# A rewritten head order, carried products over four quarters of the array, and moved transfers in a linear-attention and mixer kernel

## The chip, the cores and the metric

The kernel runs on one core of a Trainium2 chip. The metric is the device time of one execution in microseconds. TensorE (PE) multiplies, VectorE (DVE), ScalarE (ACT) and GpSimd (POOL) do the elementwise work, SyncE (SP) issues nearly all transfers, in the order of its queue.

## The reference

Three stages follow each other on 4 batches of 768 tokens with 8 heads of 48 values:

```
f = 1 / (1 + exp(-f_logit))
state = f[t] * state + k[t] (outer) v[t];  y[t] = q[t] @ state        # attention, per head
xn = (x - mean) / sqrt(var + 1e-6) * g_ln;  x = x + relu(xn @ w_ch1) @ w_ch2        # first block
h = relu(x.T @ w_tok1) @ w_tok2;  u = x + h.T                         # second block, token mixing
out = u + relu(u @ w_ch1') @ w_ch2'                                   # second block, channels 384 -> 1536 -> 384
```

Weights and activations are split into a high and a low part, and each product is made of three (high x high, high x low, low x high).

## The kernel before

**Attention** is cut into 24 chunks n of 128 tokens; chunk n has batch n mod 4 and place c = n div 4 in its sequence, so chunks 0 to 3 have no old state. The steps of a chunk are named in the order list: `lf`, `lq`, `lv` load, `log` takes the logarithm of the gate, `cum` sums it on TensorE (from chunk 8 `scan` does it on VectorE), `ek` and `eq` are the factors for K and Q, `km` and `qm` the products with them, `kp` transposes K on TensorE and `kt` copies it, `sc` are the scores, `st` the new state, `A0` and `A1` the masked scores, `stm` the state at the chunk's middle, `ste` and `std` the state at its end, `y` (L441) the products inside a half chunk, `z` (`outp2`) the **carried** products of Q with the old and the middle state (L432), `lna`, `lnc`, `lnv`, `lnr` the normalisation, `tp`, `ah`, `al` the transposed result in two parts. Scores, new states and outputs of a chunk lie in one pair of PSUM banks (`t["sc"]`). An output half i are 64 tokens and 64 of the array's columns; a row half r are four heads and 64 of the array's rows.

**First block.** Three chunks make a step `m0` to `m7` with 12 groups of 9 products of 384 columns (`m0.5`; `h` and `l` are its two parts) and 12 groups of the second layer (`m0.o21`; `r` adds and `d` stores the result). The weights `w0` to `w23` are loaded (`ld`), converted on VectorE (`a`, `b`, `c`) and split (`h`, `l`); later weights `s0`, `s1`, ... go through memory.

**Second block.** R (L852) and H (L874) are the token mixing, each with a tile `ts` of 256 KB from memory in two buffers; G (L932) and O (L985) are the two channel layers, O with weights in `w2h` and `w2l`, which `weights4` reloads in four pairs of 576 KB. `weights3` loads the six groups of G's weights. Checks of all weights (`cs`, L1137 to L1143) are strewn over the block at `spots`.

**The order.** Every step is entered in `Slots` with a slot number, and each engine runs its steps in the order of these numbers. Up to slot 77 the order is written out by hand in `ORDER`; a step `2.cum+11` issues 11 products of zeros ahead of itself into its own bank (`busy`, L540, 224 columns), and `1.y+10` issues 3 x 10 narrow ones (L449, 64 columns). `POOL` names the steps that GpSimd does in place of VectorE, `OTHER` the copies that change between ScalarE and VectorE, `AT` the results that go to the fourth one-bank buffer.

Of the kernel before, what the change touches and what calls it, by code (L numbers as in the profile page):

```python
# [51 lines left out]
ORDER = """
    0.lf 2.lf 0.log 1.lf 0.lq 2.log 3.lf 0.cum 2.cum+11 0.eq 0.ek 1.log 1.lq 0.lv 3.log 0.qm 0.km 1.cum+24 0.kp
    1.ek 0.kt 0.tot 2.eq 1.km 0.sc 0.st 0.A0 0.A1 3.cum 1.kp w14.ld w5.ld w5.a 2.ek 1.eq 0.y 0.stm 0.yw 1.qm 0.z
    1.kt 3.ek 2.tot 0.lna 1.sc 1.lv w14.a w5.b w5.c 1.tot w14.b 0.ste 0.std 5.lf 2.lq 0.lnc 1.st 1.A0 5.log w14.c
    0.tp+10 1.A1 1.y+10 2.km 5.cum 3.tot 1.stm 2.qm 2.lv 0.ah 1.yw 1.ste 1.z 3.lq 0.al 2.kp 3.km 2.sc 1.std 2.kt
    2.st 3.eq w14.h 4.lf 2.A1 6.lf 2.A0 3.qm 3.kp w14.l 1.lna 5.ek 1.lnc 4.log 5.tot w2.ld 2.y+6 2.stm w2.a 3.lv
    2.ste 3.kt w5.h w2.b 4.cum 6.log 1.tp 4.lq 3.sc 3.st 4.tot 3.A1 1.ah 4.eq 3.A0 w5.l 2.yw 2.z 2.std 1.al 3.y+9
    4.ek 2.lna 3.yw 3.stm 3.z 7.lf 2.lnc w4.ld 3.ste 7.log 4.qm 5.eq w4.a w2.c 4.km 4.kp 4.sc+4 w4.b w4.c 4.kt
    3.lna 4.lv w3.ld 3.lnc 4.st 2.tp 7.cum w4.h 4.A1 2.ah 7.ek 1.lnv 5.lq 6.cum w4.l w0.ld 3.tp 4.A0 8.lf 2.al 4.y  # L60
    4.stm 7.eq 7.tot w2.h 4.ste m0.4 5.km w3.a 4.yw 2.lnv 5.kp w1.ld w0.a 5.qm 5.lv 3.ah 5.kt w3.b w0.b w2.l 3.al
    w3.c w17.ld 4.z 5.sc 4.lna m0.5 5.st 6.eq 6.ek 6.tot w0.c w1.a w3.h w1.b 6.lq w0.h 5.A0 5.A1 m0.2 0.lnv w3.l
    w13.ld 5.y w1.c w17.a 3.lnv m0.3 5.yw m0.h5 w12.ld 9.lf w10.ld 6.lv 7.lv 5.stm m0.h4 m0.h2 6.km 4.lnc m0.l5
    m0.l4 5.z m0.l2 w1.h w1.l 5.lna 5.ste w0.l 6.qm 4.tp+7 5.lnc 6.kp 4.ah m0.0 4.al 5.tp 6.kt 5.lnv w17.b w13.a
    w13.b 6.sc w17.c m0.1 w13.c 5.ah w13.h 5.al w16.ld w12.a m0.h0 m0.h3 m0.h1 6.st m0.l3 9.log m1.2 w13.l w16.a
    m0.l1 w19.ld m1.1 8.log w17.h m1.h2 7.lq w12.b m1.0 w16.b m0.l0 w12.c 7.qm 6.A0 m1.l2 w17.l w15.ld m1.3 m1.h0
    7.km w18.ld m1.h1 w12.h 8.scan m1.h3 m1.l1 m1.l0 m1.5 7.kp m1.h5 7.kt w12.l 6.A1 w15.a m1.l5 7.sc m1.4 6.y
    w15.b w16.c 4.lnv w18.a w15.c w7.ld m1.o20 m1.o10 6.stm w18.b 8.lv 7.st 6.yw w16.h w15.h m1.h4 m1.l3 6.z 2.lnr
    m1.o00 w9.ld w15.l w18.c m1.l4 w19.a 8.tot w16.l 8.lq w8.ld 6.lna m0.o00 w10.a w19.b w19.c w10.b 6.ste 9.scan
    6.lnc w6.ld m1.o01 8.ek w18.h m1.o21 10.lv w19.h 7.A0 w10.c 5.lnr m1.o11 w18.l w19.l 3.std m0.o01 8.eq w9.a  # L70
    w6.a 7.A1 w22.ld m1.r01 m1.r11 7.y w10.h w6.b 10.lf w10.l w7.a m0.r01 w7.b w7.c w6.c w7.h 7.stm 8.km 8.qm
    m0.o20 9.ek w6.h 7.yw m0.o10 w11.ld m0.o21 10.log 7.z w7.l 8.kp w8.a 10.scan 8.kt w6.l m1.r21 m0.o11 9.tot
    w8.b 9.eq 7.lna w9.b 9.lq w8.c w11.a w9.c 7.ste 8.sc m0.7 11.lf w21.ld w20.ld w8.h 9.km m0.h7 m0.10 m0.r11
    m0.r21 w8.l w9.h m0.6 m0.h10 m0.l7 w11.b m1.6 m0.8 7.lnc 11.log w9.l w20.a w11.c m0.l10 w22.a m0.h6 8.st
    w23.ld w22.b w20.b w11.h m1.7 w22.c s0.ld m0.h8 m1.h6 m0.l6 w11.l 11.scan m0.l8 m0.9 w20.c w21.a 8.A0 m1.l6
    m0.h9 m0.l9 4.std m0.11 w22.h 10.eq w21.b 7.tp 7.ah m1.10 8.A1 8.stm 7.al w22.l w23.a w20.h m0.h11 s1.ld 9.lv
    8.y w20.l 11.lv 8.yw m1.h7 m1.11 m0.l11 m1.l7 w23.b 9.kp w23.c s0.a 8.z m1.8 m1.h10 10.lq 6.std 9.kt m1.h11
    9.qm w23.h 10.tot m1.h8 w21.c w23.l w21.h m1.l10 w21.l 7.lnv 8.lna 9.sc m1.l8 m0.o12 5.std 6.tp 8.lnc m1.l11
    11.eq m1.9 9.st 6.ah 6.lnv m1.h9 8.ste 9.A0 m1.l9 s2.ld 8.tp m0.o13 8.ah 10.ek 9.A1 m1.o02 9.y 9.stm s1.a 6.al
    m0.r13 s0.b 8.lnv s0.c 10.km 8.al m1.o03 9.yw m1.r03 9.z m0.o02 10.qm m0.o22 10.kp 11.ek m0.d1 10.sc 10.kt  # L80
    m0.o23 m0.o03 10.st m1.o12 11.lq 10.A0 9.lna 9.ste m1.o22 m0.r23 m1.o13 m0.r03 9.lnc 10.stm 10.ste 9.std s1.b
    7.std s0.h s1.c 10.std m1.r13 m1.d1 m0.d2 8.std m1.d0 m0.d0 s3.ld m1.o23 10.A1 8.lnr
""".split()
# [1313 lines left out]
```

## Time and profile before

| | |
|---|---|
| Time, median of 3 runs | 768.1 us (765.84 to 770.25) |
| Profiled execution | 766.76 us, span 765.0 us |
| PE busy | 751.5 us (98%), 7080 instructions |
| DVE busy | 503.2 us (66%) |
| ACT busy | 355.3 us (46%) |
| POOL busy | 126.5 us (17%) |
| Chain that ended last | PE 92%, DVE 3%, DMA 2%, ACT 1%, issue 1% |
| Granted TensorE clock | 0.999 of 2.4 GHz on the mean |

Matmuls are pipelined and the ends of their records are modelled, so TensorE counts as busy also where it starts its next product late; what counts is from start to start.

### The profile page before, as it was taken

To read this page: it belongs to the slowest core of one execution; us is meant where nothing else is said; L and a number is where in the kernel's file an instruction comes from. 1 tells how busy PE (TensorE), PEld (TensorE's weight loads), DVE (VectorE), ACT (ScalarE), POOL (GpSimd) and SP (SyncE) were. 2 spreads that over 40 slices of the span, in tenths; PEclk is the share of its full clock that TensorE was granted. 3 is DMA by queue.
4 is the path that set the end of the run, shared out by engine and by line. 5 is a ranking of instruction groups with operands and counts; after the bars stand their busy time and mean duration, and the time that the engine had idled before them with its cause. 6 is when DMAs were issued, how large, how long until landed. Compare 5 with 4: busy or idle time off the path is not lost.

```text
span 765.0 us, 17368 instructions
## 1 busy us (share of the span) xinstructions
PE 751.5 (98%) x7080; PEld 733.0 (96%) x7080; DVE 503.2 (66%) x920; ACT 355.3 (46%) x891; POOL 126.5 (17%) x108
## 2 busy tenths in 40 slices
PE   9899999999999999999999999999999999999997
PEld 8789999999999999999999899999999999999996
DVE  3889793787786776576245464867558663868481
ACT  6675343353545545443232342654347443656440
POOL 1334333024133330010000000101000000101010
PEclk9999999999999999999999999999999999999999
DMA  8675542467565675553349864344243534343401
GB/s 264 186 232 162 178 129 66 150 195 232 172 208 177 190 218 162 171 167 128 124 118 362 312 238 138 104 152 162 84 124 100 170 127 138 104 142 99 131 21 68
DMA packets 61561, 122.54 MB, mean 160 GB/s; under 512 B 6944, under 2 KB 27808, under 8 KB 60704
## 3 DMA queue, kind: packets, MB, share of 16 engines
q1 hardware_dynamic: 61472, 121.33, 50.5%
q8 instruction: 58, 0.95, 0.5%
q14 instruction: 31, 0.25, 0.1%
HBM read 96.93 MB, written 24.38 MB: 159 GB/s over the span
## 4 chain that ended last, share of the span: by engine, by line
PE 92%; DVE 3%; DMA 2%; ACT 1%; issue 1%; SPq 0%; DVEq 0%
PE mo L985 19%; PE mm L582 19%; PE mo L612 18%; PE mm L932 16%; PE rt L852 3%; PE ht L874 3%; PE sc L432 2%; DMA ts<-t_d 2%; PE sc L441 2%; PE sc L390 2%; PE sc L378 1%; PE tp L546 1%; PE kp L355 1%; PE cum L332 1%; PE tp L886 1%
## 5 line engine op out<-in xcount | busy, mean ns | idle before, releaser
L582 PE MATMUL mm<-wx 128*128 128x384 f32 x864 | 159.7, 338 | 0.4 <-DVE hl L601 0.2
L582 PEld LDWEIGHTS mm<-wx 128*128 128x128 f32 x864 | 148.9, 188 | 1.6 <-DVE x L631 0.5
L932 PE MATMUL mm<-xsh,wx 128*128 128x384 f32 x528 | 138.1, 335 | 0.9 <-DVE q L948 0.9
L612 PE MATMUL mo<-w2h,hh 128*128 128x384 f32 x288 | 98.9, 343 | 0.0
L985 PE MATMUL mo<-w2h,hh 128*128 128x384 f32 x288 | 97.2, 338 | 0.0
L932 PEld LDWEIGHTS mm<-xsh,wx 128*128 128x128 f32 x528 | 95.7, 188 | 1.4 <-PE mm L932 1.2
L612 PE MATMUL mo<-w2h,hl 128*128 128x384 f32 x288 | 96.5, 335 | 0.0
L985 PE MATMUL mo<-w2l,hh 128*128 128x384 f32 x288 | 96.3, 335 | 0.0
L612 PE MATMUL mo<-w2l,hh 128*128 128x384 f32 x288 | 96.3, 334 | 0.0
L985 PE MATMUL mo<-w2h,hl 128*128 128x384 f32 x288 | 96.3, 334 | 0.0
L932 PE MATMUL mm<-xsl,wx 128*128 128x384 f32 x264 | 88.2, 334 | 0.0
L972 POOL TENSOR_TENSOR hl<-u,hh 128x768 fp32r<-128x768 f32 x16 | 29.6, 1849 | 340.1 <-ACT u L967 277.0
L597 ACT ACTIVATE hh<-mm 128x384 fp32r<-128x384 f32 x96 | 45.9, 486 | 73.0 <-PE mm L582 72.6
L601 DVE SCALAR_TENSOR_TENSOR hl<-mm,hh 128x384 fp32r<-128x384 f32 x96 | 52.4, 552 | 24.3 <-ACT hh L597 23.8
L989 DVE TENSOR_TENSOR xr<-mo,xr 128x384 f32<-128x384 f32 x48 | 26.7, 556 | 53.6 <-PE mo L985 53.5
L1143 ACT ACTIVATE cs<-cs 128x384 f32<-128x384 f32 x56 | 31.1, 555 | 59.4 <-DVE cs L1140 59.2
L612 PEld LDWEIGHTS mo<-w2h,hh 128*128 128x128 f32 x288 | 54.1, 188 | 0.5
L985 PEld LDWEIGHTS mo<-w2h,hh 128*128 128x128 f32 x288 | 54.1, 188 | 0.1
L612 PEld LDWEIGHTS mo<-w2l,hh 128*128 128x128 f32 x288 | 54.1, 188 | 0.0
L985 PEld LDWEIGHTS mo<-w2l,hh 128*128 128x128 f32 x288 | 54.1, 188 | 0.0
L985 PEld LDWEIGHTS mo<-w2h,hl 128*128 128x128 f32 x288 | 54.1, 188 | 0.0
L612 PEld LDWEIGHTS mo<-w2h,hl 128*128 128x128 f32 x288 | 54.1, 188 | 0.0
(170 smaller groups left out, 1318.0 us busy)
## 6 DMA issues: line engine op xcount, KB each, us to landing
cs<-in_w SPq DMA_DIRECT2D x48, 384.0 KB, 3.3
sg<-in_w SPq DMA_DIRECT2D x44, 384.0 KB, 4.4
ts<-t_d SPq DMA_DIRECT2D x48, 256.0 KB, 3.0
wx<-f_d SPq DMA_DIRECT2D x6, 1152.0 KB, 12.4
V<-in_v_n SPq DMA_DIRECT2D x21, 288.0 KB, 4.3
T<-in_k_t SPq DMA_DIRECT2D x21, 224.0 KB, 2.9
T<-in_q_t SPq DMA_DIRECT2D x21, 224.0 KB, 3.6
x_d<-x SPq DMA_DIRECT2D x24, 192.0 KB, 2.7
```

The lines of the kernel that those rows point to most:

```text
L390: nc.tensor.matmul(t["sc"][64 * r:64 * r + w, i, o:o + D], t["kt"][half(i), P2 * p + 64 * r:P2 * p + 64 * r + w], t["V"][half(i), D * h:D ...
L582: nc.tensor.matmul(ps, w[:, f, k, :], x[:, k, :], start=(i == 0), stop=(i == 8))
L597: nc.scalar.activation(out=hid(f)[0], in_=t[f], func=AF.Relu)
L601: nc.vector.scalar_tensor_tensor(hl, t[f], 0.0, hh.bitcast(F32), op0=ALU.max, op1=ALU.subtract)
L612: nc.tensor.matmul(ps, x, w[:, f, :], start=(f == lo and i == 0), stop=(f == hi and i == 2))
L852: nc.tensor.matmul(t["r"][j], w, x, start=(s == 0 and i == 0), stop=(s == NCH - 1 and i == 2))
L874: nc.tensor.matmul(ps, w, x[:, j], start=(i == 0), stop=(i == 5))
L932: nc.tensor.matmul(ps, w, x, start=n == 0, stop=n == len(ops) - 1)
L972: le.tensor_tensor(l, whole(g, i), h.bitcast(F32), op=ALU.subtract)
L985: nc.tensor.matmul(ps, x, w[:, f], start=(g % 3 == 0 and m == 0 and n == 0), stop=(g % 3 == 2 and m == 1 and n == 2))
L989: nc.vector.tensor_tensor(us[b, u], t["o", u], us[b, u], op=ALU.add)
L1143: nc.scalar.activation(out=t["u"], in_=t["u"], func=AF.Abs, accum_out=wlow[:, i:i + 1])
```

## The change

The head's order list is replaced, with the same steps in it; its sets of engines and buffers change with it. It holds 56 wide zero products in the old list (11, 24, 10, 4 and 7) and 23 in the new (4, 4, 9, 3 and 3), and 75 and 9 narrow ones. The carried products of a chunk with old state go round the four quarters of the array in place of half by half. Two pairs of second-block weights, two stores, the H products, the transposes ahead of G and the last batch's checks get other slots.

```diff
 POOL = set("""
-    1.qm 0.std 3.km 3.qm w14.l w5.l 4.km w4.l w3.l 6.km w0.l 6.qm w13.l w17.l w12.l w15.l w18.l w19.l 3.std w10.l
-    8.km w7.l 9.km w9.l 4.std w22.l w20.l 9.qm w23.l w21.l 5.std 10.qm 8.std 11.km 11.qm 11.std
+    1.km 2.km 2.qm 3.qm w3.l 0.std 4.qm w5.l 1.std w0.l w1.l 6.km w2.l w4.l 7.km w16.l 2.std w14.l w12.l 4.std
+    w15.l w10.l w6.l w8.l 9.km 9.qm w22.l 11.km 11.qm 11.std
 """.split())
 ORDER = """
-    0.lf 2.lf 0.log 1.lf 0.lq 2.log 3.lf 0.cum 2.cum+11 0.eq 0.ek 1.log 1.lq 0.lv 3.log 0.qm 0.km 1.cum+24 0.kp
-    1.ek 0.kt 0.tot 2.eq 1.km 0.sc 0.st 0.A0 0.A1 3.cum 1.kp w14.ld w5.ld w5.a 2.ek 1.eq 0.y 0.stm 0.yw 1.qm 0.z
-    1.kt 3.ek 2.tot 0.lna 1.sc 1.lv w14.a w5.b w5.c 1.tot w14.b 0.ste 0.std 5.lf 2.lq 0.lnc 1.st 1.A0 5.log w14.c
-    0.tp+10 1.A1 1.y+10 2.km 5.cum 3.tot 1.stm 2.qm 2.lv 0.ah 1.yw 1.ste 1.z 3.lq 0.al 2.kp 3.km 2.sc 1.std 2.kt
-    2.st 3.eq w14.h 4.lf 2.A1 6.lf 2.A0 3.qm 3.kp w14.l 1.lna 5.ek 1.lnc 4.log 5.tot w2.ld 2.y+6 2.stm w2.a 3.lv
-    2.ste 3.kt w5.h w2.b 4.cum 6.log 1.tp 4.lq 3.sc 3.st 4.tot 3.A1 1.ah 4.eq 3.A0 w5.l 2.yw 2.z 2.std 1.al 3.y+9
-    4.ek 2.lna 3.yw 3.stm 3.z 7.lf 2.lnc w4.ld 3.ste 7.log 4.qm 5.eq w4.a w2.c 4.km 4.kp 4.sc+4 w4.b w4.c 4.kt
-    3.lna 4.lv w3.ld 3.lnc 4.st 2.tp 7.cum w4.h 4.A1 2.ah 7.ek 1.lnv 5.lq 6.cum w4.l w0.ld 3.tp 4.A0 8.lf 2.al 4.y
-    4.stm 7.eq 7.tot w2.h 4.ste m0.4 5.km w3.a 4.yw 2.lnv 5.kp w1.ld w0.a 5.qm 5.lv 3.ah 5.kt w3.b w0.b w2.l 3.al
...
+    0.lf 0.log 0.cum 1.lf 1.log 0.lq 0.ek 0.eq 1.cum+4 2.lf 0.lv 0.km 2.log 0.kp+4 0.qm 0.kt 1.eq 3.lf 1.ek 0.tot
+    0.sc 1.lq w3.ld 1.tot 0.st 3.log 0.A1 0.A0 2.cum 0.stm 3.cum+9 1.qm 3.ek 0.y 3.tot 0.yw 1.km w3.a 0.z 2.ek
+    2.eq 0.lna 1.sc+3 1.lv 2.lq w3.b 4.lf 1.kp w3.c 1.kt w5.ld 5.lf 1.st 0.ste 3.lq 0.lnc 1.A1 1.A0 2.km 1.stm
+    0.tp+3 2.tot 3.eq 2.kp 1.y+3 4.log 2.qm 3.qm w5.a 0.lnv 1.yw 1.z 2.sc 0.ah 2.kt 4.cum 5.log 1.lna w5.b 0.al
+    3.km 3.kp 2.lv 3.lv w3.h 4.lq 1.lnc 1.ste 2.st w5.c 2.A0 2.A1 1.tp 3.sc w3.l 0.std 4.ek w5.h 5.cum 1.ah w0.ld
+    2.stm 2.y 4.eq 3.kt 5.eq 3.st 1.al 4.km 2.ste 3.A0 2.yw 2.z 4.qm 3.A1 3.y w0.a 6.lf 5.ek 4.kp 2.lna 7.lf 3.yw
+    6.log 3.stm 2.lnc 4.lv w0.b 3.z w5.l 4.sc 7.log 5.tot 2.tp 4.kt w0.c 4.st w1.ld 6.cum w0.h 7.cum 3.ste 2.ah
+    w1.a 3.lna 1.std 4.stm 4.A0 7.tot 4.A1 4.y 7.eq 6.tot 2.al 4.yw w1.b w4.ld 1.lnv 4.tot 5.lq w2.ld w1.c 5.qm
+    m0.5 5.km w1.h w0.l 4.z w2.a 3.lnc 4.ste w16.ld m0.0 w1.l 5.lv 6.eq 6.ek 5.kp 7.ek 5.kt w4.a 5.sc 2.lnv 3.tp
...
-LATER = dict(log=-12.25, lq=-12.75, qm=-6.5, lnc=7.5, kt=-6.25, tp=11.55)
+LATER = dict(log=-12.25, kt=-6.25, tp=11.55, lq=-12.75, qm=-6.5, lnc=7.5)
...
-JOBS = [15.20, 19.00, 22.30, 28.10, 31.40, 37.20, 40.00,
...
+JOBS = [15.20, 19.00, 22.30, 28.10, 31.40, 36.20, 40.00,
...
 AT = set("""
-    cum0 kp1 tp0 cum4 tp2 m0.4 kp6 m0.1 m1.0 m1.4 o000 kp8 m0.7 m0.8 m0.11 kp9 o011 o021
+    cum0 kp1 cum4 m0.0 kp6 tp4 m1.5 o000 o100 m0.11 m0.9 m1.9 o101 o111
 """.split())
 OTHER = set("""
-    1.stm 2.kt w14.h 3.kt w5.h 3.stm w16.h w7.h 8.kt w22.h w20.h 10.kt
+    0.kt 0.stm 1.kt 2.kt 2.stm 3.kt 4.kt w16.h w14.h w19.h w6.h w8.h 10.kt
 """.split())
...
             eng("std").tensor_tensor(s, s, decs[:P2, n].rearrange("p (a o) -> p a o", o=1).to_broadcast([P2, NP, D]),
                                      op=ALU.mult)
-        def carried(i):
-
-
-            s = t["S"][1] if i else old()
+        def carried():
+
+
             for p in range(NP):
-                for r in range(2):
+                for r, i in ((0, 0), (1, 1), (1, 0), (0, 1)) if c else ((0, 1), (1, 1)):
+                    s = t["S"][1] if i else old()
                     nc.tensor.matmul(t["sc"][half(i), r, D * p:D * p + D], t["Q"][rows(r), p, half(i)],
                                      s[rows(r), D * p:D * p + D], start=False, stop=p == NP - 1)
...
         def outp2():
             block = nc.cur_bb.bb
             z = len(block.instructions)
-            if c:
-                carried(0)
-            carried(1)
+            carried()
             follow(block.instructions[z], t["done"])
         def heads(x):
...
                 sl.p(q, lambda z=0, u=u, g=g: mm2(u, g, z), f"{m}o{u}{g}")
                 if g == 3 or pair and g == 1:
                     sl.late(q + 1, lambda u=u: fin(u, t["o", u]), f"{m}r{u}{g}")
+            q = MP2 + 2 * u - 1.7 if step == N1 - 1 and u else q
             sl.late(q + 1, lambda u=u: out(u), f"{m}d{u}")
     def fin1(step):
...
     for g in range(6):
         sl.e(S7 + FT + 2 + .5 * g, lambda g=g: weights3(g))
     for i, f in enumerate((0, 6, 3, 9)):
-        sl.e(MP2 + (2, 4, 16, 18)[i], lambda f=f: weights4(f, 3))
+        sl.e(MP2 + (6.5, 8.3, 16, 18)[i], lambda f=f: weights4(f, 3))
     def tokmix(b):
         t = {}
...
     sl.e(S7 + 9.6, T0["rr_e"])
     sl.late(S7 + 9.6, T0["rr_l"])
     for i in range(3):
-        q = S7 + 11 + 1.4 * i
+        q = S7 + 10.6 + 2.2 * i
         for j in range(2):
             sl.e(q - 2.5 + j, lambda i=i, j=j: T0["lt"](1, i + 3 * j))
             sl.p(q + j / 2, lambda i=i, j=j: T0["hh"](i + 3 * j))
             mixed(T0, i + 3 * j, q + j / 2 + .5)
-        sl.p(S7 + 16 + 1.2 * i, lambda i=i: T0["tr"](i))
-        xmix(T0, i, S7 + 16.4 + 1.2 * i)
+        sl.p(S7 + 17 + 1.2 * i, lambda i=i: T0["tr"](i))
+        xmix(T0, i, S7 + 17.4 + 1.2 * i)
     def double(b, cur):
         Z = strassen(b)
...
             times[step[:3] if f == O else step[:2]] = cur
             cur = f(*a)
         lo, hi = times[O, 0, 0], cur - 1 if b < B - 1 else cur - 16
-        lo = lo if b < B - 1 else times[G, 0] + 1
+        lo = lo if b < B - 1 else times[G, 0] + .2
         spots.extend(lo + (hi - lo) * i / 14 for i in range(14))
         return cur
```

## Rows read from the trace of the kernel before

**Rows 1.** Busy time by stretch: us from:to, length, engines, granted clock, DMA share, GB/s
```profile
10.00:40.00 30.00, 26.46 (x723) 23.36 (x720) 20.91 (x45) 18.99 (x58) 9.58 (x8) 1.00 0.73 221
40.00:70.00 30.00, 29.97 (x443) 27.52 (x434) 28.05 (x58) 19.91 (x57) 10.19 (x10) 1.00 0.65 201
100.00:350.00 250.00, 249.78 (x3142) 242.53 (x3141) 177.21 (x346) 116.38 (x305) 62.53 (x53) 1.00 0.56 174
...
759.40:765.00 5.60, 0.00 (x0) 0.00 (x0) 0.56 (x1) 0.00 (x0) 0.00 (x0) 0.80 0.13 46
```

**Rows 2.** Groups by line and shape, TensorE: count, busy us, mean ns, idle before
```profile
L540 PE MATMUL cum<-zeros 128*128 128x224 bf16 x35 | 3.7, 259 | 0.0
...
L449 PE MATMUL sc<-zeros 128*128 128x64 bf16 x75 | 2.7, 193 | 1.1 <-DVE A L400 0.9
```

**Rows 3.** Timeline of TensorE, head: start us, length us, what, count
```profile
8.46 2.46 PE L540 MATMUL cum<-zeros 128*128 128x224 bf16 x24
...
11.64 0.55 PE L355 MATMUL kp<-ident,first 112*128 112x112 f32 x4
...
40.13 1.83 PE L582 MATMUL mm<-wx 128*128 128x384 f32 x9
```

**Rows 4.** Timeline of VectorE, head: the first chunk's K product
```profile
8.69 0.69 DVE L343 TENSOR_TENSOR first<-first,ek 112x512 f32<-112x512 f32 x1
```

**Rows 5.** Timeline of TensorE, chunks 18 and 21 (inner, scores, carried products)
```profile
274.30 0.68 PE L441 MATMUL sc<-V,A 64*64 64x48 f32 x32
274.80 0.66 PE L378 MATMUL sc<-T 48*64 48x64 f32 x32
...
275.73 0.47 PE L432 MATMUL sc<-state,T 48*64 48x48 f32 x10
...
276.19 0.46 PE L432 MATMUL sc<-mid,T 48*64 48x48 f32 x10
...
322.65 0.25 PE L432 MATMUL sc<-state,T 48*64 48x48 f32 x1
...
323.21 0.46 PE L432 MATMUL sc<-mid,T 48*64 48x48 f32 x10
```

**Rows 6.** Instructions of line 432: count, ns min/median/max, first to last start
```profile
L432 PE MATMUL sc<-state,T x320: 218/218/253, 42.3 to 353.7; 48*64 48x48 f32 x160
```

**Rows 7.** Groups by line and shape, 0 to 130 us, GpSimd and VectorE
```profile
L253 POOL TENSOR_TENSOR w2l<-cu,w2h 128x384 fp32r<-128x384 f32 x11 | 13.3, 1215 | 29.8 <-ACT w2h L248 19.6 <-DVE w2h L246 10.2
...
L253 DVE TENSOR_TENSOR wx<-cu,wx 128x384 fp32r<-128x384 f32 x5 | 3.0, 604 | 0.0
```

**Rows 8.** Waits of TensorE: waiting line, releaser, us in total, times, longest
```profile
PE rt L852 <- DMA ts<-t_d: 1.2, 2, 0.7
...
PE mm L932 <- DVE q L948: 0.9, 1, 0.9
...
PE sc L432 <- DVE mid L246: 0.6, 1, 0.6
PE sc L432 <- ACT mid L248: 0.5, 1, 0.5
...
PE ht L874 <- DMA ts<-t_d: 0.2, 1, 0.2
```

**Rows 9.** Timeline of SyncE's queue, 400 to 445 us: loads and stores issued
```profile
403.67 2.46 SPq L812 DMA_DIRECT2D wx<-f_d  x5
...
421.03 0.32 SPq L634 DMA_DIRECT2D x_d<-x  x1
...
426.77 0.38 SPq L817 DMA_DIRECT2D w2h<-h_d  x1
...
442.35 0.32 SPq L807 DMA_DIRECT2D ts<-t_d  x1
```

**Rows 10.** Chain that ended last, 425 to 460 us: start us, length us, what
```profile
428.88 7.31 DMA ts<-t_d
...
450.17 9.36 PE mo L985 x54
```

More of the change, by code (lines that the diff above doesn't have):

```diff
@@ L59 @@
-    4.ek 2.lna 3.yw 3.stm 3.z 7.lf 2.lnc w4.ld 3.ste 7.log 4.qm 5.eq w4.a w2.c 4.km 4.kp 4.sc+4 w4.b w4.c 4.kt
-    3.lna 4.lv w3.ld 3.lnc 4.st 2.tp 7.cum w4.h 4.A1 2.ah 7.ek 1.lnv 5.lq 6.cum w4.l w0.ld 3.tp 4.A0 8.lf 2.al 4.y
-    4.stm 7.eq 7.tot w2.h 4.ste m0.4 5.km w3.a 4.yw 2.lnv 5.kp w1.ld w0.a 5.qm 5.lv 3.ah 5.kt w3.b w0.b w2.l 3.al
-    w3.c w17.ld 4.z 5.sc 4.lna m0.5 5.st 6.eq 6.ek 6.tot w0.c w1.a w3.h w1.b 6.lq w0.h 5.A0 5.A1 m0.2 0.lnv w3.l
-    w13.ld 5.y w1.c w17.a 3.lnv m0.3 5.yw m0.h5 w12.ld 9.lf w10.ld 6.lv 7.lv 5.stm m0.h4 m0.h2 6.km 4.lnc m0.l5
@@ L64 @@
[L64 to L82, printed above, removed]
+    0.lf 0.log 0.cum 1.lf 1.log 0.lq 0.ek 0.eq 1.cum+4 2.lf 0.lv 0.km 2.log 0.kp+4 0.qm 0.kt 1.eq 3.lf 1.ek 0.tot
@@ new lines @@
+    6.log 3.stm 2.lnc 4.lv w0.b 3.z w5.l 4.sc 7.log 5.tot 2.tp 4.kt w0.c 4.st w1.ld 6.cum w0.h 7.cum 3.ste 2.ah
+    w1.a 3.lna 1.std 4.stm 4.A0 7.tot 4.A1 4.y 7.eq 6.tot 2.al 4.yw w1.b w4.ld 1.lnv 4.tot 5.lq w2.ld w1.c 5.qm
+    m0.5 5.km w1.h w0.l 4.z w2.a 3.lnc 4.ste w16.ld m0.0 w1.l 5.lv 6.eq 6.ek 5.kp 7.ek 5.kt w4.a 5.sc 2.lnv 3.tp
+    5.st w16.a w2.b w16.b w2.c m0.h0 w4.b m0.1 6.lq 5.A1 5.A0 m0.h5 3.ah w14.ld 5.stm m0.l5 m0.l0 w16.c 6.qm 4.lna
+    5.y m0.3 6.km w13.ld 5.yw 5.z 4.lnc 3.al m0.h1 w2.h 3.lnv 6.kp 6.kt w2.l 5.lna 6.lv w17.ld w4.c 6.sc m0.2
@@ new lines @@
+    m0.l1 w14.a 4.tp w15.ld w16.h w14.b w4.h 5.lnc w4.l m0.h3 m0.l3 4.ah w14.c 4.al 6.st 5.tp 5.ah m0.4 m0.h4
+    m0.h2 5.al w13.a w14.h 7.lq 7.km 6.A0 w13.b m1.5 w16.l 8.lv 9.lf m0.l2 w12.ld m1.2 m1.3 w12.a 6.A1 2.std m0.l4
+    3.std m1.h2 m1.l2 w12.b 6.y 7.qm m1.h3 2.lnr w14.l w12.c 9.log w12.h m1.1 w15.a w7.ld 7.lv m1.h1 w13.c w12.l
+    m1.4 5.ste w13.h m1.l3 m1.l1 6.yw 7.sc m1.h4 w15.b w13.l 7.kp w19.ld w11.ld w17.a m1.h5 7.kt w17.b w15.c w15.h
+    4.std m1.0 w17.c w15.l m1.h0 m1.l4 m0.o20 7.st w17.h 6.stm m0.o10 w10.ld 8.lf m1.l0 w17.l 7.A0 w7.a m1.l5
@@ new lines @@
+    8.log w7.b w11.a w11.b 9.scan 6.z w10.a 9.tot 8.scan w7.c 8.eq 9.lv 6.ste w11.c 8.tot w7.h 7.A1 m1.o10 m0.o00
+    8.ek w11.h m1.o11 8.lq m0.o11 m0.o01 8.qm w7.l 4.lnv 8.km w10.b 6.lna 7.y m0.r11 w8.ld 5.lnv m0.o21 m1.7 w19.a
+    5.lnr m0.r01 w9.ld w10.c m0.r21 m1.r11 m1.o00 9.eq w10.h w19.b w10.l w11.l w6.ld w6.a m1.o20 w19.c 6.lnc w6.b
+    w9.a 8.kp w9.b m1.o21 9.ek w6.c w19.h w19.l w8.a w8.b w6.h w9.c w20.ld m1.r21 s0.ld w22.ld 8.sc 7.yw 10.lf
+    8.kt m1.o01 m1.r01 8.st m1.11 m1.h7 m1.h11 w9.h 8.A1 w6.l w22.a w22.b w8.c 7.stm 11.lf 7.ste w18.ld w21.ld
@@ new lines @@
+    10.log m1.6 m0.11 m0.h11 7.z w8.h m1.l11 m1.l7 w9.l m0.6 6.std 9.lq w18.a w18.b w8.l w20.a 9.km m1.h6 w18.c
+    m0.7 8.A0 w18.h w20.b w23.ld m0.l11 m0.h6 11.log m0.9 w22.c w18.l w20.c m0.h7 m0.l7 m1.l6 7.lna w20.h m0.l6
+    m0.h9 w21.a m1.8 m0.8 w21.b m0.l9 8.y 9.qm w20.l 9.kp 8.stm 7.lnc 10.scan w23.a m1.9 m0.h8 9.kt 8.yw m1.h8
+    m1.l8 w23.b 10.ek m1.h9 w21.c m1.10 9.sc m0.l8 m1.h10 8.z w23.c 10.lq s1.ld 10.lv 9.st 8.lna s2.ld m1.l9 5.std
+    w23.h 10.eq m0.10 w21.h w23.l 11.scan w21.l m0.o22 m0.h10 w22.h m0.l10 8.ste m1.o02 m1.l10 10.qm 9.A1 7.tp
@@ L83 @@
+    7.ah w22.l 6.tp m1.o03 7.lnv 9.A0 7.al 9.y 8.lnc 8.tp m1.r03 m0.o23 11.ek 6.lnv 11.eq 10.tot 10.km s0.a 7.std
+    9.yw m1.o12 s1.a 8.lnv 6.ah 9.stm 8.std m0.r23 m1.d0 m0.d2 9.z s0.b 10.sc 10.kp 6.al 8.ah 8.al m0.o02 9.lna
+    10.kt 9.ste m0.o12 9.std s0.c m1.o22 m0.o13 10.st 9.lnc 10.stm s1.b 11.lq m0.r13 m0.o03 s1.c 10.A1 m0.r03
+    m1.o13 10.A0 10.ste m1.r13 m0.d1 m0.d0 m1.o23 10.std s3.ld 11.lv m1.d1 8.lnr s0.h
 """.split()
-LATER = dict(log=-12.25, lq=-12.75, qm=-6.5, lnc=7.5, kt=-6.25, tp=11.55)
+LATER = dict(log=-12.25, kt=-6.25, tp=11.55, lq=-12.75, qm=-6.5, lnc=7.5)
@@ L91 @@
 """.split())
-JOBS = [15.20, 19.00, 22.30, 28.10, 31.40, 37.20, 40.00, 43.30, 47.60, 50.40, 55.20, 59.00, 63.80, 66.10, 69.40, 72.20, 78.00, 81.30, 87.60, 89.40, 92.70, 98.00, 99.30, 104.10, 107.40, 111.70, 115.50, 117.80]
+JOBS = [15.20, 19.00, 22.30, 28.10, 31.40, 36.20, 40.00, 43.30, 47.60, 50.40, 55.20, 59.00, 63.80, 66.10, 69.40, 72.20, 78.00, 81.30, 87.60, 89.40, 92.70, 98.00, 99.30, 104.10, 107.40, 111.70, 115.50, 117.80]
 AT = set("""
-    cum0 kp1 tp0 cum4 tp2 m0.4 kp6 m0.1 m1.0 m1.4 o000 kp8 m0.7 m0.8 m0.11 kp9 o011 o021
+    cum0 kp1 cum4 m0.0 kp6 tp4 m1.5 o000 o100 m0.11 m0.9 m1.9 o101 o111
 """.split())
 OTHER = set("""
-    1.stm 2.kt w14.h 3.kt w5.h 3.stm w16.h w7.h 8.kt w22.h w20.h 10.kt
+    0.kt 0.stm 1.kt 2.kt 2.stm 3.kt 4.kt w16.h w14.h w19.h w6.h w8.h 10.kt
 """.split())
```

## The prediction

> **What bounds the kernel now.** I read the busy time by stretch first, to see which engine is full where; then TensorE's timeline in the first 60 us; then the waits of TensorE, the chain of waits and SyncE's queue around 420 us. The reader is to see three things. From 100 to 350 us TensorE is idle for 0.2 us in all, at a granted clock of 1.00 [rows 1]; there only fewer or faster TensorE instructions shorten the run. From 10 to 40 us TensorE is busy for 26.46 of 30 us, and part of that is filler: multiplications of zeros that the order writes in as "+N" [rows 1, 2]. From 40 to 70 us TensorE is full, but so nearly is VectorE, with 28.05 of 30 us [rows 1]. The remaining waits of TensorE are few and short [rows 8].
>
> **Part 1, carried products.** Nothing is added or removed: a chunk with old state (n = 4 to 23, 20 chunks: 320 products of the state at 16 a chunk [rows 6]) still issues 32 products of 48 x 64 x 48. Before, 16 go to output half 0, alternating the two row halves of the array, then 16 to half 1. After, each head pair visits (row half, output half) = (0,0), (1,1), (1,0), (0,1), which is the sequence of the inner products of L441. The trace shows what each pace costs. The 32 products of L441 take 0.68 us from the first start to the last end; the carried 32 run from 275.73 to 276.19 + 0.46 = 276.65, so 0.92 us; in a later chunk from 322.65 to 323.21 + 0.46 = 323.67, so 1.02 us [rows 5]. The scores, with the 48 rows that the carried products have, take 0.66 us for 32 and 64 columns [rows 5], so 48 rows are no obstacle. I count 16 chunks like the first and four (19 to 22) like the second: 16 x 0.24 + 4 x 0.34 = 3.8 + 1.4 = 5.2 us. Sixteen of the chunks stand behind 100 us, where TensorE is full, so theirs counts whole; the other four lie between 42 and 90 us, where it may meet VectorE. Bounds: 0 (if the pace is one per instruction whatever the quadrant) and 20 x (1.02 - 0.66) = 7.2 us. I take 5.2, since the row of L441 is the same sequence.
> The Trainium skill ("TensorE: Matmul & The Clock Gate", section "Wait — 56ns, not 53.3ns?") says that start-to-start never drops below about 25 ns however small the product is; 32 x 25 = 0.8 us would leave nothing to save. By that rule the part is worth 0. The trace disagrees: L441 has 32 done in 0.68 us [rows 5], 21 ns each with the last one's whole length in it, and the row decides.
> The edit also adds a wait: the first carried product now needs the middle state too, which only the second half needed. All of TensorE is queued behind it. What hid a late middle state was the first half, at most 0.46 us. The waits on the middle state are 0.6 and 0.5 us, once each [rows 8]; where the middle state is later than the old one the cost lies between 0 and 20 x 0.46 us. I take 0, because both waits listed are of chunks without old state (their source is the copies of L246 and L248), and no wait on L413's sum stands in the list.
>
> **Part 2, the order of the head.** By counting in the two lists: ahead of the first 384-wide group (m0.4 before, m0.5 after) stand the same TensorE steps, 8 sums, 5 transposes of K, 5 scores, 5 state products, 5 inner and 4 carried products, and 3 transposes of the normalised chunk in place of 4. What differs is filler. The wide filler falls from 56 to 23 instructions, the narrow one from 75 to 9. A run of 24 lasts 2.46 us [rows 3], one alone 0.26 [rows 2], so the pace is (2.46 - 0.26) / 23 = 0.096 us; the narrow ones take 2.7 / 75 = 0.036 us [rows 2]. That is 33 x 0.096 + 66 x 0.036 = 3.2 + 2.4 = 5.6 us of filler removed. It is worth that only where something useful comes sooner, as filler stands where TensorE would wait.
> Where it does: the first transpose of K starts at 11.64, directly behind the 24 fillers and a sum [rows 3]; its operand was ready at 8.69 + 0.69 = 9.38, although VectorE did Q ahead of K [rows 4]. After, K is loaded ahead of the third chunk's gates, ScalarE makes its factor first, VectorE does K first, and 8 fillers remain; the transpose comes at 8.3 to 9.4, so 2.3 to 3.3 us sooner. The first 384-wide group starts at 40.13 [rows 3]. Up to that group the old order spends 49 x 0.096 + 75 x 0.036 = 7.4 us on filler and 3.5 us idle (30 - 26.46 [rows 1]); the new one has 23 x 0.096 + 9 x 0.036 = 2.5 us of filler. If all idle time went as well the group would come 4.9 + 3.5 = 8.4 us sooner: the upper bound. ScalarE, whose steps ahead of the group are about the same, is busy for 18.99 us of these 30 [rows 1]; in 30 - 8.4 it would be 88% full, which speaks for less.
> Against it: engines swap work. Counted from the sets, VectorE gets four more low parts of weights, two more copies of K^T, one more gate product and one more decay, less one weight copy. A low part costs 0.60 us there against 1.22 on GpSimd [rows 7]; at that length the seven more are 4.2 us, while VectorE has 2 us to spare between 40 and 70 us. What is late next is thus VectorE: part of what is gained at 40 us is given back by 90 us. Lower bound: fillers turn into waits one for one and VectorE's 4 us come on top, a loss of 4 us. I take 4.0 us of gain: 5 at the first group (less than the 8.4, about the filler removed) less 1 given back.
> The changed set of buffers (AT) and the order's moved loads have no row of their own; I count them into these bounds.
>
> **Part 3, the turn to the second block.** Before, the store of chunk 22 waits in SyncE's queue until 421.03 and holds up all loads behind it [rows 9]. After, it and the next store stand behind the first four loads. That gains little, as the six 1152 KB loads issued from 403.67 on [rows 9] keep the transfers full and the small ones land behind them; and spreading the H products puts the fourth of them, which the last load ahead waits for, one group further back, which lets those six loads start about 1 us later. I count +0.3 us for the first R group. Spreading gives each H tile longer to land and removes the wait of H: -0.2 [rows 8]. Moving the two pairs of 576 KB loads from 426.77 [rows 9] to behind the fifth and sixth R tiles clears the way of the third, which took 7.31 us from issue to landing [rows 10]: -0.9 of the 1.2 us that R waits [rows 8]. The second pair is then issued behind the tile of 442.35 [rows 9] and is needed at 450.17 [rows 10], 7.8 us on, more than the 7.31 us that a tile took in the crowd [rows 10]. Transposes for the mixing come one group later; I see 0 to 0.4 us of wait there. Moving the checks of the last batch earlier may take away or move the wait of 0.9 us on VectorE's q [rows 8]: half of it, -0.5. Sum: 0.3 - 0.2 - 0.9 + 0.4 / 2 - 0.5 = -1.1; bounds -2.6 and +2 (a late second pair).
>
> **Sum.** -5.2 - 4.0 - 1.1 = -10.3 us. The profiled execution took 766.76 us (span 765.0), which gives 756.5. The median shown is 768.1, 1.3 above the profiled one; I take half of that: 757 us, 1.4% faster.
>
> **Rivals.**
> A. The filler only hid waits. TensorE then stands where fillers were, and Part 2 is worth 0: 766.76 - 5.2 - 1.1 = 760.5, with the offset 761. For it: VectorE and ScalarE are chained chunk by chunk in the head. Against it: the transpose at 11.64 waited for filler alone.
> B. The head gains all of 8.4 and Part 3 2.6: 766.76 - 5.2 - 8.4 - 2.6 = 750.6, with the offset 751. Against it is VectorE between 40 and 70 us.
> C. The carried products do not speed up, the change then not doing what it says: 757 + 5.2 = 762.2.
> D, the other side: with less filler TensorE's clock falls in the head. The granted clock is 1.00 from 10 to 40 us, idle time included, and averages 0.80 over the 5.60 us behind the last product, where TensorE does nothing [rows 1]: rest does lower it to 1.2 GHz. At half clock the work between 8 and 40 us, some 19 us without filler, would take 19 us more: 757 + 19 = 776. It decides once over 10.3 us of that work runs at the low level. Against it: 3.5 us of idle time spread over 30 us left the clock at 1.00, and the useful products stand closer together after the change.
> The Trainium skill ("TensorE: Matmul & The Clock Gate", section "HAM oscillation — how this bites in real kernels") tells of kernels whose clock falls to half in waits between bursts. The stretch from 10 to 40 us shows no such fall [rows 1]; no run here has the head without its filler.
> E. VectorE's extra 4 us come through whole and eat Part 2: 766.76 - 5.2 + 4 - 1.1 = 764.5, with the offset 765, no change.
>
> **Chances.** Forecast 0.56, A 0.19, B 0.12, C 0.05, D 0.04, E 0.04. Within 0.5% (764.3 to 771.9) is what this measurement cannot tell from no change. Faster by more: nearly all of forecast, B and C, and most of A, together 0.88; the same 0.08; slower 0.04, D. The range of 8 in 10 reaches from B to the upper half of A and C: 750.5 to 763.5.
>
> **What would show it.** Right: the 32 carried products take about 0.68 us; the first 384-wide group starts at 34 to 37 us; the granted clock stays 1.00; the 576 KB loads stand behind the sixth R tile and R waits for no tile but the first. Wrong: TensorE's waits in 10 to 100 us grow by what filler fell; VectorE is full from 30 to 90 us and ends TensorE's waits; the second product group of the second block waits for w2h.

## The result, and the profile after

The kernel after takes 757.09 us (median of 4, 755.31 to 762.48) where the kernel before took 767.46 beside it (4, 765.84 to 770.25): a ratio of 0.9866, 95% interval 0.9834 to 0.9898. The forecast was 757.0. The profiled execution took 755.93 us with a span of 754.2, 10.8 less than that of before. The total was right, two terms behind it were not: the head gave more than its 4.0 us, and the turn to the second block cost time where it was to save some.

Busy time by stretch of the kernel after (columns as in [rows 1]):
```profile
10.00:40.00 30.00, 27.26 (x670) 23.75 (x663) 23.36 (x50) 21.80 (x67) 12.56 (x11) 1.00 0.83 239
40.00:70.00 30.00, 30.00 (x457) 27.26 (x456) 28.09 (x61) 16.38 (x42) 11.82 (x12) 1.00 0.67 202
100.00:350.00 250.00, 249.29 (x3197) 242.44 (x3196) 179.50 (x350) 118.36 (x312) 55.93 (x46) 1.00 0.56 175
```
TensorE is fuller in the head (27.26 us of 30, before 26.46 with more filler in it), at full clock in this execution. VectorE is as busy from 40 to 70 us as before (28.09 against 28.05), and from 100 to 350 us TensorE is full as it was: what was won there comes from shorter sequences of products, not from idle time (0.71 us in these 250, before 0.22).

Timeline of TensorE in the kernel after: the first transpose of K, the first 384-wide group, and the first and last rows of the carried products of one chunk:
```profile
8.48 0.55 PE L538 MATMUL kp<-zeros 128*128 128x224 bf16 x4
8.89 0.57 PE L355 MATMUL kp<-ident,first 112*128 112x112 f32 x4
...
35.65 0.62 PE L580 MATMUL mm<-wx 128*128 128x384 f32 x2
...
266.43 0.24 PE L432 MATMUL sc<-mid,T 48*64 48x48 f32 x2
...
266.87 0.29 PE L432 MATMUL sc<-state,T 48*64 48x48 f32 x4
```
The transpose is 2.75 us sooner than in [rows 3], the first group 4.48. The carried products run from 266.43 to 267.16, 0.73 us where [rows 5] had 0.92 and 1.02. In the trace `mid` and `state` now alternate, as the diff says.

Waits of TensorE in the kernel after:
```profile
PE rt L851 <- DMA ts<-t_d: 2.7, 2, 1.6
...
PE sc L432 <- ACT done L456: 1.0, 3, 0.3
...
PE mm L931 <- DVE q L941: 0.2, 1, 0.2
```
The wait on `q` is down from 0.9 us, the waits of H are gone, but R waits 2.7 us for its tiles (before 1.2) [rows 8]. The chain that ended last, at the first and around the sixth R tile of the second batch, and SyncE's queue around the sixth, in the kernel after:
```profile
399.85 17.11 DMA ts<-t_d
...
431.18 4.07 DMA ts<-t_d
435.25 0.14 issue
435.38 1.30 PE rt L851 x6
436.68 3.65 PE mm L931 x21
440.33 4.68 PE mo L984 x27
```
```profile
426.50 0.32 SPq L806 DMA_DIRECT2D ts<-t_d  x1
426.87 0.43 SPq L816 DMA_DIRECT2D w2h<-h_d  x1
427.35 0.42 SPq L816 DMA_DIRECT2D w2l<-h_d  x1
427.82 0.43 SPq L831 DMA_DIRECT2D xr<-x_d  x1
431.18 0.32 SPq L806 DMA_DIRECT2D ts<-t_d  x1
431.55 0.43 SPq L816 DMA_DIRECT2D w2h<-h_d  x1
```
The first tile, issued behind the six 1152 KB loads, lands 17.11 us later. The first moved pair of 576 KB loads is issued right behind the fifth tile (426.87) and ahead of the sixth (431.18); that tile takes 4.07 us to land, and TensorE waits 1.1 us for it.

By place, the two profiled executions differ as follows (a landmark is the start of a product that both kernels have):

| landmark | before, us | after, us | difference |
|---|---|---|---|
| first 384-wide group | 40.13 | 35.65 | -4.48 |
| third step's first group | 140.08 | 132.64 | -7.44 |
| eighth step's first group | 372.05 | 361.15 | -10.90 |
| first O product | 450.01 | 440.17 | -9.84 |
| behind the last batch's first checks | 701.29 | 690.46 | -10.83 |
| last product | 759.06 | 748.15 | -10.91 |

Between the second and the third row 14 chunks give 3.46 us, 0.247 each. The turn gives 1.06 back, the last batch's checks take off 0.74.

### The profile page after: what moved, and what is told of

It is laid out like the page before. It is cut to its first block, busy times and chain, and to the rows that moved or that the text cites. A ratio compares the mean times of both kernels' runs of the same rounds, so it can differ in the third digit from the quotient of the medians.

```text
span 754.2 us, 17189 instructions
## 1 busy us (share of the span) xinstructions
PE 741.1 (98%) x6981; PEld 723.0 (96%) x6981; DVE 502.9 (67%) x927; ACT 355.5 (47%) x890; POOL 119.5 (16%) x102
## 4 chain that ended last, share of the span: by engine, by line
PE 90%; DMA 4%; DVE 3%; ACT 2%; issue 1%; SPq 0%; DVEq 0%; ACTq 0%
PE mo L984 20%; PE mo L610 18%; PE mm L580 18%; PE mm L931 17%; PE rt L851 3%; PE ht L873 3%; DMA ts<-t_d 3%; PE sc L441 2%; PE sc L432 1%; PE sc L378 1%; PE sc L390 1%; PE tp L544 1%; PE kp L355 1%; PE tp L885 1%; DMA firstv<-in_w 1%; PE warm L734 1%
```

## The experiments

**The carried products alone**, in the kernel before:
```diff
-        def carried(i):
...
-            s = t["S"][1] if i else old()
...
-                for r in range(2):
+        def carried():
...
+                for r, i in ((0, 0), (1, 1), (1, 0), (0, 1)) if c else ((0, 1), (1, 1)):
+                    s = t["S"][1] if i else old()
...
```


> The kernel before with the carried products alone going over the four quarters. Theory (the quarters work at once, so the 32 products of a chunk take some 0.7 us in place of 0.9 to 1.0): each of the 20 chunks gains about 0.25 us, 16 of them for sure as TensorE is full behind 100 us. Time 5 us less than before (about 0.993 of it), the trace behind 360 us 5 us earlier, waits elsewhere as before. Rival (the new rate is only used up where the head order is changed too, or the gain ends in waits on ScalarE and VectorE): under 2 us.

Measured: 762.7 us (7 executions, 761.0 to 765.59), ratio 0.9931 (0.9911 to 0.9951), which is 5.3 us of 767.5, between 3.8 and 6.8. In the trace the end comes 4.99 us sooner, 3.66 of it between the first groups of the third and of the eighth step. From first to last start the carried products of the 20 chunks take 14.64 us before and 9.96 here, 4.7 less. The term of 5.2 us holds, and the rival of under 2 us is out.

**The head alone** (`ORDER`, `POOL`, `AT`, `OTHER` of after in the kernel before; the one store that moves in `JOBS` stays at its old slot, here and in all experiments on the kernel before):

> The kernel before with the new order, engine sets and buffers of the head alone. Theory (the head is a chain, and filler and queue places lengthened it): the first 384-wide group starts 4 to 5 us earlier and 140 us of before is reached 5.5 to 6 us earlier; time 6 us less (0.992). Rival A (filler only hid waits; what moved the head was the carried products): under 2 us. Granted clock 1.00 in the head by both; a clock below it would speak for the rival that filler kept the clock up.

Measured: 760.15 us (5, 758.9 to 763.59), ratio 0.9906 (0.9873 to 0.9939): 7.2 us, between 4.7 and 9.7. Its profiled execution took 761.68 us; the first 384-wide group stands in the timeline of TensorE at
```profile
35.18 1.86 PE L582 MATMUL mm<-wx 128*128 128x384 f32 x9
```
4.95 us sooner than in [rows 3], and the difference is 4.99 us at the third step's first group and 4.97 at the end. VectorE gives nothing back, and rival A's under 2 us is out.

**The turn alone** (weight pairs, H products, transposes and two stores; the checks stay):
```diff
+            q = MP2 + 2 * u - 1.7 if step == N1 - 1 and u else q
-        sl.e(MP2 + (2, 4, 16, 18)[i], lambda f=f: weights4(f, 3))
+        sl.e(MP2 + (6.5, 8.3, 16, 18)[i], lambda f=f: weights4(f, 3))
-        q = S7 + 11 + 1.4 * i
+        q = S7 + 10.6 + 2.2 * i
...
-        sl.p(S7 + 16 + 1.2 * i, lambda i=i: T0["tr"](i))
+        sl.p(S7 + 17 + 1.2 * i, lambda i=i: T0["tr"](i))
...
```


> The kernel before with the moved transfers of the second block alone (two stores, the H products, the transposes ahead of G, two pairs of 576 KB loads). Theory: it costs. The first R tile lands behind six loads of 1152 KB that start later, and the sixth R tile behind the first moved pair: about 1 us more from the H products to the first O product than before (54.6 us from 395.45 to 450.01 before), time +1 us, within the noise of the timing. Rival (as predicted): 0.6 us less in that stretch, the waits of the changed kernel coming from its being ahead elsewhere.

Measured: 768.71 us (10, 767.26 to 771.35), ratio 1.0018 (1.0000 to 1.0036): no gain, a cost of 0 to 2.8 us. From the first H product to the first O product it takes 55.42 us, before 54.56. Waits of TensorE from 375 us on:
```profile
PE rt L853 <- DMA ts<-t_d: 2.5, 2, 2.0
PE mm L933 <- DVE q L949: 1.0, 1, 1.0
```
The H waits are gone and R waits 2.5 us in place of 1.2 [rows 8], as in the kernel after.

**The kernel after with the old turn**, first executed once, then timed beside the kernel after itself:
```diff
-            q = MP2 + 2 * u - 1.7 if step == N1 - 1 and u else q
-        sl.e(MP2 + (6.5, 8.3, 16, 18)[i], lambda f=f: weights4(f, 3))
+        sl.e(MP2 + (2, 4, 16, 18)[i], lambda f=f: weights4(f, 3))
-        q = S7 + 10.6 + 2.2 * i
+        q = S7 + 11 + 1.4 * i
...
-        sl.p(S7 + 17 + 1.2 * i, lambda i=i: T0["tr"](i))
+        sl.p(S7 + 16 + 1.2 * i, lambda i=i: T0["tr"](i))
...
```


> The changed kernel with the transfers at the turn to the second block (two stores, the H products, the transposes ahead of G, two pairs of 576 KB loads) as they were before. Theory (the moved transfers cost, as the first and sixth R tile show): from the first H product to the first O product some 54.6 us in place of the 55.6 of the changed kernel, all else as there. Rival (the changed kernel would wait there with the old places too, as it is 11 us ahead of its transfers): 55.5 us or more.

> The kernel after, with the four moves of the turn undone (second-block weight pairs, H products, transposes, two stores), now timed. Theory: the moves cost time in every execution, 1.5 to 2.3 us between the first H product and the first product of the second output layer; the median is 755 to 755.8 us, 1.3 to 2 us under the kernel after in the same call, and from the first H product to the first O product it takes 53.0 to 53.8 us (55.6 with the moves). Rival: the gain of the single look was one execution's luck in when loads land; the median is then that of the kernel after within 0.5 us, and that stretch takes 54.6 us or more.

> The kernel after once more, beside the run with the old turn. Theory: 756.8 to 757.5 us, ratio to the kernel before 0.986 to 0.988; first H product to first O product 55.3 to 55.9 us. Rival: if the turn's length depends on the execution more than on the order, that stretch comes out at 54.6 us or less here and the two medians are the same.

Executed once: 754.53 us. Timed: 756.52 us (5, 754.29 to 757.76), ratio 0.9851 (0.9826 to 0.9875), beside the kernel after with 757.74 (5, 756.98 to 761.22), ratio 0.9868 (0.9845 to 0.9890). The medians stand 1.2 us apart in the direction expected, less than expected, and the intervals overlap: the times alone don't show it. The traces bear it out. From the first H product to the first O product the seven profiled executions with the old turn take 53.29 to 54.78 us (mean 53.97), the five with the new one, without the next experiment, 54.64 to 56.43 (mean 55.49); the two sets overlap by 0.14 us. The two runs timed here have 53.72 and 56.43, the latter outside its expected 55.3 to 55.9: in it TensorE runs at 1.2 GHz from 421.50 to 424.91 us, right after 1.7 us of waiting for the first R tile, which by itself can lengthen the stretch by up to 1.7 us (an estimate: half of these 3.41). Without this execution the mean of the new turn is 55.25, still 1.3 above the old. Waits of TensorE from 375 us on with the old turn:
```profile
PE rt L850 <- DMA ts<-t_d: 0.4, 1, 0.4
PE mm L930 <- DVE q L940: 0.3, 1, 0.3
PE ht L872 <- DMA ts<-t_d: 0.2, 1, 0.2
```
and with the new one, in the execution of 761.22 us:
```profile
PE rt L851 <- DMA ts<-t_d: 2.0, 2, 1.7
PE mm L931 <- DVE q L941: 0.5, 1, 0.5
```

**Later weights.** Three of the six groups of G's weights and two of O's pairs go behind the R tiles:
```diff
-        sl.e(S7 + FT + 2 + .5 * g, lambda g=g: weights3(g))
+        sl.e(S7 + FT + 2 + .5 * g if g < 3 else MP2 + 18.1 + .3 * g, lambda g=g: weights3(g))
-        sl.e(MP2 + (6.5, 8.3, 16, 18)[i], lambda f=f: weights4(f, 3))
+        sl.e(MP2 + (2.3, 5.2, 23.5, 24)[i], lambda f=f: weights4(f, 3))
```


> The changed kernel with other places for weights of the second block: the last three of the six 1152 KB loads behind the second H tile of the second batch, the first two pairs of 576 KB behind the third and the fourth R tile, the other two pairs 6 to 8 slots later. Theory (R waits because its tiles lie behind 7 MB of G's weights, half of it not needed for 40 us, and the sixth behind a pair): R's waits, 2.7 us in the list, fall under 0.5, and the stretch from the first H product to the first O product from 55.6 to some 53.3 us; time 2 us less than the changed kernel. Rival (the transfers are full in this stretch whatever the order, so the wait moves to the O products or to the later H tiles): less than 1 us.

Measured: 761.79 us (8, 757.76 to 764.82), ratio 0.9922 (0.9897 to 0.9947), slower than the kernel after's 0.9868 (0.9845 to 0.9890). Waits of TensorE from 375 us on:
```profile
PE ht L873 <- DMA ts<-t_d: 3.1, 1, 3.1
PE rt L851 <- DMA ts<-t_d: 1.6, 1, 1.6
```
The waits moved with the loads. With three of the six 1152 KB loads behind it, the first R tile is not waited for any more; the two pairs now stand behind the third and the fourth R tile, and it is the fifth that is 1.6 us late, not the sixth; and a later H tile of the same batch, now behind the three moved groups of G, is 3.1 us late. From the first H product to the first O product it takes 54.49 us, 1.1 less than in the kernel after, and from there to the last product 3.1 us more. Part of the lost time lies in the head, which the edit leaves alone: the first 384-wide group stands at 40.38 us in this execution, 4.7 later than in the kernel after. **The same with two head loads drawn forward** (`w1.ld w2.ld` right behind `w0.ld`):

> As the kernel with the other places for the second block's weights, and in the head's order the loads of w1 and w2 moved ahead of two gate loads that wait for a buffer. Theory (in the changed kernel VectorE stands still for 1.24 us at 32.1 to 33.3 for w1, whose load waits in SyncE's queue behind such a load, and the fifth chunk's masked scores stand behind it): the first 384-wide group starts about 1 us earlier, at 34.5 to 35, and half to all of that is still there at 140 us; time 2.5 to 3 us less than the changed kernel. Rival (VectorE is the head's bound and takes the time back): nothing left at 140 us.

Measured: 764.1 us (10, 760.24 to 768.18), ratio 0.9956 (0.9931 to 0.9980). H waits 3.6 us, and the first 384-wide group comes at 36.87 us, later than after's 35.65 and not sooner. Neither edit shows a gain; as two executions of the kernel after have this group at 35.65 and 39.46, one execution can't say what the drawn-forward loads do by themselves.

**The filler.** All "+N" left out, from the kernel before and from the kernel after; the zero products add nothing to the result.
```diff
-    0.lf 2.lf 0.log 1.lf 0.lq 2.log 3.lf 0.cum 2.cum+11 0.eq 0.ek 1.log 1.lq 0.lv 3.log 0.qm 0.km 1.cum+24 0.kp
+    0.lf 2.lf 0.log 1.lf 0.lq 2.log 3.lf 0.cum 2.cum 0.eq 0.ek 1.log 1.lq 0.lv 3.log 0.qm 0.km 1.cum 0.kp
...
```


> The kernel before without the zero products of the head order (56 wide and 75 narrow ones left out; the 28 at the very start stay). Theory: some of the filler was in the way: the first K transpose starts at 9.4 to 9.8 in place of 11.64, and the first 384-wide group 2 to 3 us earlier, the rest of the 7.4 us turning into waits. Rival A (filler only hid waits): the group stays within 1 us of 40.13. Rival D (filler keeps TensorE's clock up): the granted clock falls under 1.00 between 10 and 40 us, and the time grows by over 5 us.

> The changed kernel without the zero products of the head order (23 wide and 9 narrow ones left out). Theory (after the old order without filler the clock fell to half twice between 19 and 43 us: filler holds the clock, and the new order is dense enough that little of it is needed): the clock stays at 1.00 or falls in one stretch only, the first 384-wide group starts between 35 and 38 us. Rival (the new order's useful work alone holds the clock, so its filler costs what it lasts): clock 1.00 all through and the group 1 to 2 us before 35.65. Rival D in full: two falls as in the old order and the group over 4 us late.

> The kernel before without its filler, again and timed (zero products ahead of the head's steps left out; the result is not touched by them). Theory: without filler TensorE's clock falls in the head in every execution, so the time is 768 to 770 us and the profile shows a stretch of 6 us or more at half clock between 10 and 45 us. Rival: the two falls seen began behind waits of 2.6 and 1.9 us for blocks of TensorE's own instructions that landed late in that one execution; where no such wait is longer than 1 us the clock stays at 1.00, the first 384-wide group starts at 36 to 40 us and the median is 763 to 767 us.

Executed once each: 769.4 us and 755.97 us. Timed, before without filler takes 766.91 us (10, 764.3 to 769.83), ratio 0.9983 (0.9961 to 1.0005): neither the 768 to 770 of my theory nor a gain that shows. The granted clock averages 0.986 to 0.996 in these ten executions, 0.991 to 1.000 in those of the kernel before. Timeline rows of TensorE that begin behind an unnamed wait, in the first execution of before without filler, and busy time by stretch:
```profile
19.13 0.79 PE L390 MATMUL sc<-firstv,kt 64*64 64x48 f32 x24 [2.58 <-issue]
33.46 0.33 PE L390 MATMUL sc<-V,kt 64*48 64x48 f32 x9 [1.88 <-issue]
```
```profile
20.00:30.00 10.00, 9.06 (x170) 7.51 (x171) 6.45 (x16) 4.86 (x15) 3.76 (x3) 0.69 0.51 154
30.00:40.00 10.00, 6.90 (x204) 5.86 (x203) 6.72 (x17) 6.23 (x19) 2.46 (x2) 0.82 0.66 197
```
The clock stands at 1.2 GHz from 19.30 to 26.13 and from 36.37 to 43.19 us, each time after TensorE had stood. So rival D's mechanism is real in a head without filler; what the filler costs and what it saves come out about even. My rival's condition (no wait over 1 us) did not occur in the second profile either: a wait of 1.83 us and two stretches at 1.2 GHz.

The kernel after without filler went as my theory had it: the clock falls once, from 17.45 to 24.28 us, and the first 384-wide group starts at 36.42. With no filler in either, the old order has this group at 44.55 and 41.59 us: it is the new order that brings the group forward, not the missing filler, as far as three executions show it.

**Another order of the quarters, and the checks back at their old slot**:
```diff
-                for r, i in ((0, 0), (1, 1), (1, 0), (0, 1)) if c else ((0, 1), (1, 1)):
+                for r, i in ((0, 0), (1, 0), (0, 1), (1, 1)) if c else ((0, 1), (1, 1)):
...
-        lo = lo if b < B - 1 else times[G, 0] + .2
+        lo = lo if b < B - 1 else times[G, 0] + 1
```


> The kernel after with two separate edits, read in two stretches. (1) The carried products visit the quarters (row half, output half) in the order (0,0), (1,0), (0,1), (1,1), so that every second step stays in its output half. If it is the use of four quarters in turn that counts, the 32 products still start within 0.46 us; if each step must change its output half, 16 steps at the old pace of 0.70/31 = 0.023 us and 15 at 0.015 us give 0.59 us, and the end comes 14 x 0.13 = 1.8 us later from 100 to 372 us; if only the old alternation of row halves counts, 0.70 us. (2) The last batch's checks start at their old slot. Theory: the wait of the last batch's first layer on VectorE's q comes back, 0.7 to 0.9 us between its products 396 and 450; rival: that wait was of the executions, and the stretch stays at 14.5 us as after (15.2 before).

Measured: 761.94 us, once. Timeline of TensorE, first and last rows of one chunk's carried products:
```profile
271.95 0.25 PE L432 MATMUL sc<-mid,T 48*64 48x48 f32 x2
...
272.40 0.28 PE L432 MATMUL sc<-state,T 48*64 48x48 f32 x3
```
and a wait of the last batch:
```profile
PE mm L931 <- DVE q L947: 0.9, 1, 0.9
```
The 32 products of this chunk start within 0.51 us, as those of the chunk shown for the kernel after do, and from the third to the eighth step's first group it is as long (228.48 against 228.51): the four quarters in turn count, not which of these two orders they come in. The wait on `q` is back, and its stretch takes 15.26 us (after 14.49, before 15.23). The late total is the head's again: the first 384-wide group stands at 41.30 us.

## Why the prediction held, step by step

- **Carried products, -5.2.** Right: -5.3 timed alone, -4.99 in the trace, 4.7 by the starts alone. The row of L441 priced it, a little high: most chunks take 0.73 us, not its 0.68. Before, 32 starts took 0.70 us and more; after, 0.42 to 0.54. That a start never comes sooner than 0.025 us, as the Trainium skill has it ("TensorE: Matmul & The Clock Gate", section "Wait — 56ns, not 53.3ns?"), the runs contradict once more: 0.51 us over 31 steps is 0.016. No wait for the middle state's sum came with it; the rows name ScalarE's `done` for 1.0 us.
- **The head, -4.0.** The forecast of 5 at the first group and its main step, the transpose of K 2.3 to 3.3 us sooner, came as worked out (4.48 and 2.75). The term that was mis-sized is the 1 us that VectorE was to give back: alone, the head keeps 4.99 us at the third step's first group, and gains 7.2 by the medians. In the kernel after, the two parts together gain more by that group than each alone there (7.44 against 4.99 and 0.85); 0.9 us of it is two unnamed waits that the head alone has between 36 and 140 us and the kernel after has not, the rest stays open.
- **Clock at 1.00.** Right in the profiled execution, not in general. The same kernel, profiled again, has 1.2 GHz from 32.38 to 39.20 us and its first group at 39.46. Of its nine executions six have a mean clock of 0.991 to 0.996; of the 49 of the kernel before that stand beside these runs, eleven. Rival D decides nothing, but a fall of the clock, which it names, is there in most executions of the kernel after; where in the kernel it lies is known only for the two that were profiled.
- **The turn, -0.6 without the checks.** This is the step that failed. "Moving the two pairs of 576 KB loads from 426.77 to behind the fifth and sixth R tiles clears the way of the third" was true of the third: it comes 0.15 us sooner relative to the first H product. But behind the fifth is ahead of the sixth, and I asked of the moved pairs only whether they are late themselves. The sixth tile's products start 1.0 us later relative to the first H product, and the first tile's 0.66, not 0.3. "R waits for no tile but the first" is refuted. The other executions say the same and show where most of the cost lies: with the new turn the first tile is waited for 1.3 to 2.1 us in all five, with the old one 0.54 at most in all seven; the sixth 0.3 to 1.1 us in all five, in none of the seven; the third in none of the five, and 0.7 to 0.9 us in three of the seven. On the means the first tile's products start 0.9 us later, and the sixth adds 0.7. So the term for the first R group was mis-sized, and the one for the third was worth its price in some executions only. That it is the pairs which delay the sixth agrees with the later weights: with the pairs behind the third and fourth tile, the fifth waits. And the 0.2 us of H in [rows 8] was a tile of the second batch, at 471 us, that the spread H products of the first batch don't touch. In all, +1.06 between the first H product and the first O product in the two profiles, +1.5 on the mean of twelve; timed alone, 0 to 2.8. What the two stores and the transposes do by themselves was not tried.
- **The checks, -0.5.** 0.74 in this profile, where nearly all of the wait on `q` went (0.9 to 0.2). In the seven profiled executions with the new slot its stretch takes 14.48 to 15.05 us (mean 14.66), in the seven with the old one 15.23 to 15.27: 0.6 on the mean, rather more than half of the wait of 0.9. Putting the slot back brings the wait back.

The errors of head and turn have opposite signs, and that the sum came out to 0.1 us is luck; a single total would have hidden both. The best version run is the kernel after with the old turn, 756.52 us, though its lead on the kernel after is within the intervals.

## What to carry to other kernels

Small products over quarters of the array cost least here when all four quarters are in turn (0.42 to 0.54 us for 32 starts, 0.70 and more over two), in both orders tried: look in the timeline for sequences that stay in one half. A load that is moved behind one urgent transfer stands ahead of the next: for each move list what is issued behind it until it has landed, not only who needs it. And a head should be judged over several executions, since one profile may show it at its best: the kernel after has its first 384-wide group at 35.65 us in one and at 39.46 in the next.
